# Conditioned block with cached attention and a gated mixer: w4's load keyed apart from w3's, the last tile's norm ahead of the first w2 product's passes, the second pair's attention outputs loaded by halves of heads

## The chip, the cores and the metric

The kernel runs on one core of one Trainium2 chip. The metric is the device time of one launch in microseconds (us); the time of a kernel is the median of its runs. The profile is that of one execution; its span runs from the first to the last instruction.

## What is computed

`x` has 2048 rows of 640. With `D = 640`, 32 heads of 128, 2048 cached keys and values per head and `F = 1728`:

```python
mod = silu(c) @ w_mod                       # six rows: sa, ca, ga, sb, cb, gb
h = layernorm(x) * (1 + ca) + sa
q = (h @ wq) split into 32 heads of 128
o = softmax(q @ k_cache.T * 128**-0.5) @ v_cache
x = x + ga * (o @ wo)                       # wo: 4096 x 640
h = layernorm(x) * (1 + cb) + sb
g = gelu(layernorm(h) @ w1)                 # 640 x 640; then each quarter of the
                                            # columns shifted by 1, -1, 2, -2 rows
x1 = h + shifted(g) @ w2                    # 640 x 640
y = x1 + gelu(layernorm(x1) @ w3) @ w4      # w3: 640 x 1728, w4: 1728 x 640
out = x + gb * y
```

Operands are bf16, sums fp32.

## The kernel before

**Order.** A small planner (`Prog`) takes operations in the order in which the code names them, puts each on its engine's list, and derives the waits from named keys: an operation waits for the last writer of every key it reads or writes, and for the readers of every key it writes. Each engine runs its list in order, and a transfer's wait is taken by the engine that issues it: whatever stands behind it on that engine waits too. There is no other scheduler; the order of the code is the order on every engine.

**Attention.** Most of the time goes into 512 steps (one head, one tile of 128 query rows): scores on PE, minimum and negation on DVE (L584), exponential on ACT (L597), a DMA transpose of the probabilities (L230), and the product with the values on PE (L307). GpSimd normalizes the outputs and writes them to a scratch in DRAM (L462), grouped by pairs of query tiles (tiles 0 and 1 are pair 0, tiles 2 and 3 pair 1, and so on).

**The part behind it.** The 16 tiles of 128 rows pass through these stages. I name them as the code does:

- `load_ot(pr)` (L504): SP issues a DMA transpose that brings a pair's 32 heads (64 blocks of 128 x 128) from the scratch into one of two buffers, `hTx` for even pairs and `negS` for odd ones. Pair 0 comes in three pieces (12, 12 and 8 heads), every other pair in one. The key `("OT", buffer, part)` has three parts, and a whole load writes all three. Pair 1 is issued at L623, behind pair 0's last piece and the first quarter of x (`load_xt(0, 1)`, L622); the rest of x follows at L625, and pair 2 with the loads of w1 and w2 after that (L731 to L734).
- `a_pe(j)` (L523): PE multiplies tile j's 32 heads by `wo`: 32 matmuls of 512 columns and 32 of 128 into one of two PSUM banks (L532). `parts` and `hs` let it do some heads only. A bank comes free when DVE has read it (`a_s1`, L644).
- `a_s1`, `a_s2` (L642, L650): DVE adds the product to x, normalizes, modulates and takes the statistics of the next norm; two small GpSimd operations (`rs_of`, L629) make the reciprocal root.
- `nrm_of(l, j)` (L660): DVE writes the normed tile into one of two buffers (L666), and SP issues a DMA transpose of it into `nT` (L672). l is 1 ahead of w1 and 2 ahead of w3.
- `b_op(cc, n)` (L698): five matmuls of w1 for four tiles (L703) into one of two other PSUM banks, and on ACT the GELU that empties the bank (one to three ACTIVATEs, L711). The first eight of the 20 are placed between parts of the last two tiles' `a_pe` (L742, L745).
- `c_op(j)` (L757): ten matmuls of w2 for a tile (L765), DVE's add (L769), statistics, and `nrm_of(2, j-1)`.
- `d_op` (L774): five matmuls of w3 (L780) and a GELU on ACT; `e_op` (L816): 28 matmuls of w4 (L829), DVE, and the output's store.

**Around the change.** When the last tile's `a_s2` has been listed, GpSimd clears two small pads (L751, L752), and ACT issues the loads of w3 (L753) and of w4's first 13 blocks (L754). Both go into the memory that `wo` held, and both write the key `"wo"`, which every `a_pe` reads. Then come `b_op(1, 3)` and `b_op(1, 4)` (L841), and the loop of L855: `c_op(0)`, `nrm_of(1, 15)` (L858), two `b_op`s, `c_op(1)`, two `b_op`s, `c_op(2)`, the load of w4's last block (L860, on SP, which also writes `"wo"`), one `b_op`, `c_op(3)`, and so on. So on PE the order is b(1,3), b(1,4), c(0), b(2,0), b(2,1), c(1), b(2,2), b(2,3), c(2), b(2,4), c(3), b(3,0), b(3,1), c(4), b(3,2), b(3,3), c(5), b(3,4), c(6), d(0,0). b(3,n) needs `nT` of tiles 12 to 15, d(0,n) needs w3 and `nT` of tiles 0 to 3 in their second form.

Of the kernel before, what the change touches and what calls it, by code (L numbers as in the profile page):

```python
# [123 lines left out]
def bass_adaLN_cond__mha_block_cached__mixer_s_mlp__prompt_kernel(  # L124
# [3 lines left out]
    _, H, SK, DH = A_k_cache.shape  # L128
    FF = B_w3.shape[1]
    assert DH == 128 and D % 128 == 0 and SQ % 512 == 0 and SK == 2048  # L130
    KT = D // 128
    NQT = SQ // 128
    NQC = SQ // 512
    NKT = SK // 128
    NFT = (FF + 127) // 128
    FL = FF - (NFT - 1) * 128
# [9 lines left out]
    with ExitStack() as es:  # L146
# [11 lines left out]
        if True:  # L158
            with ExitStack() as es1:
# [8 lines left out]
                wo = sb1("wo", [128, H, D], BF16)  # L168
# [40 lines left out]
                G = Prog(nc, es1, "a")  # L209

                def load_k(h):
                    hb = h % 2
                    G.dma("sync", lambda e: e.dma_start_transpose(KTs[:, hb], A_k_cache[0, h]), ("k", hb), w=[("KT", hb)])
# [126 lines left out]
                if H > 1:  # L340
                    load_wq(1)
                    load_k(1)
                G.dma("sync", lambda e: e.dma_start(wo[:], A_wo.rearrange("(h p) n -> p h n", p=128)), "wo", w=["wo", "woz"])

                G.op("gpsimd", lambda g: g.memset(ident[:], 0.0), w=["id0"])
                G.op("gpsimd", lambda g: g.memset(ones_f, 1.0), w=["onesf"])
# [2 lines left out]
                     r=["id0"], w=["ident"])  # L349
# [3 lines left out]
                for k in range(KT):  # L353
                    G.op("gpsimd", lambda g, k=k: g.tensor_scalar(out=s_bc[:, k, :], in0=ones_f, scalar1=c_f[:, k:k + 1],
                                                                  scalar2=1.0, op0=ALU.mult, op1=ALU.mult),
                         r=["onesf", "cf"] + WRK, w=[("sbc", k)])
# [129 lines left out]
                w4 = wof[:, KT * NFT * 128:KT * NFT * 128 + NFT * D].rearrange("p (f n) -> p f n", f=NFT)  # L486
# [10 lines left out]
                NEG = [("negS", i) for i in range(3)]  # L497
                KVK = ([("KT", b) for b in range(2)] + [("V", b) for b in range(2)] + [("wq", b) for b in range(2)]
                       + [("QT", b, cc) for b in range(2) for cc in range(NQC)])
                HTK = [("hT", cc, k) for cc in range(NQC) for k in range(KT)]  # L500
# [3 lines left out]
                def load_ot(pr, h0=0, h1=H, part=0):  # L504
                    G.dma("sync", lambda e: e.dma_start_transpose(
                        OTj[pr % 2][:, 2 * h0:2 * h1, :], o_scr[pr, :, h0:h1].rearrange("q h z d -> q (h z d)")),
                          ("ot", pr % 2, part), r=[("osd", pr // 2, hh) for hh in range(h0, h1)],
                          w=[("OT", pr % 2, i) for i in ([part] if h1 - h0 < H else range(3))]
                          + ((HTK if pr == 0 else NEG) if pr < 2 else []))

                def load_xt(c0, c1):
                    G.dma("sync", lambda e: e.dma_start(
                        xt[:, 4 * c0:4 * c1], x2d[c0 * 512:c1 * 512, :].rearrange("(t p) d -> p t d", p=128)),
                        ("xt", c0), w=[("x1", t) for t in range(4 * c0, 4 * c1)] + ringk(XT0 + 4 * c0 * D, XT0 + 4 * c1 * D))
# [4 lines left out]
                def ybank():  # L519
                    yn[0] += 1  # L520
                    return yn[0] % 2

                def a_pe(j, b=None, parts=(0, 1, 2), hs=None):  # L523
                    if b is None:
                        b = ybank()
                    pr, z = divmod(j, 2)
                    h0, h1 = hs or (OTC[parts[0]], OTC[parts[-1] + 1])

                    def f(t):
                        for c0, cw in NC2:  # L530
                            for hh in range(h0, h1):
                                ins = t.matmul(YB[b][:, c0:c0 + cw], OTj[pr % 2][:, 2 * hh + z, :], wo[:, hh, c0:c0 + cw],  # L532
                                               start=(hh == 0), stop=(hh == H - 1))
                        return ins
                    G.op("tensor", f, r=[("OT", pr % 2, i) for i in parts] + ["wo", "woz"], w=[("S", b)])
                    return b

                YB = [Sps[:, 0:1024], Sps[:, 1024:2048]]
                LAG = 4
                for s in range(NG + PVD + LAG):  # L540
                    h, j = divmod(s, NQT)
# [5 lines left out]
                    if s == 3:  # L547
                        G.op("gpsimd", lambda g: g.tensor_scalar(
                            out=mod_bc[:, 2 * D:3 * D], in0=mod_bc[:, 2 * D:3 * D], scalar1=1.0, scalar2=1.0, op0=ALU.add, op1=ALU.mult),
                            r=[("mod", i) for i in range(len(MROW))], w=["mod"])  # L550
                    for half in range(2):
                        if s < NG:
                            qk(s, half)
                        if half == 0 and s in (NG + PVD - 5, NG + PVD - 4):
                            b0 = a_pe(0, None if s == NG + PVD - 5 else b0, (s - NG - PVD + 5,))
                        if half == 0 and s == NG + PVD - 2:
                            b1 = a_pe(1, None, (0,))
# [15 lines left out]
                    if 0 <= g_ < NG and g_ % 2 == 1:  # L573
                        p = g_ // 2
                        G.op("scalar", lambda a, p=p: a.copy(  # L575
                            Of[:, p % 4].rearrange("p z d -> p (z d)")[:, 0:259], PO[:, (p % 2) * 512:(p % 2) * 512 + 259]),
                            r=[("O", p % 2)], w=[("Of", p % 4)])
# [3 lines left out]
                    for half in range(2):  # L581
                        if s < NG:
# [6 lines left out]
                                r=[("S", half)], w=[("negS", s % 3), ("nmh", half, r8)])  # L589
# [3 lines left out]
                    if s < NG:  # L593
                        G.op("gpsimd", lambda g, r8=r8: g.tensor_scalar(  # L594
                            out=nm[:, r8:r8 + 1], in0=nm0[:, r8:r8 + 1], scalar1=nm1[:, r8:r8 + 1], scalar2=None, op0=ALU.min),
                            r=[("nmh", 0, r8), ("nmh", 1, r8)], w=[("nm", r8)])
                        G.op("scalar", lambda a, s=s, r8=r8: a.activation(  # L597
                            Pb[:, s % RP, :], negS[:, s % 3, :], ACT.Exp, bias=nm[:, r8:r8 + 1], scale=-1.0),
                            r=[("negS", s % 3), ("nm", r8)], w=[("Pb", s % RP)])
# [7 lines left out]
                        if h + 1 == H and j in (2, PVD + 1):  # L607
                            i = 0 if j == 2 else 1
# [10 lines left out]
                    if s == NG:  # L619
                        G.op("gpsimd", lambda g: g.memset(mhalf, -0.5), w=["mhalf"] + NEG)  # L620
                        load_ot(0, OTC[2], OTC[3], 2)
                        load_xt(0, 1)  # L622
                        load_ot(1)  # L623
                    if s == NG + 2:
                        load_xt(1, NQC)  # L625
                GELU = ACT.Gelu_apprx_tanh
# [23 lines left out]
                def a_s2(j):  # L650
                    u = j % 2
                    G.op("vector", lambda v: v.scalar_tensor_tensor(out=tmp[:, u], in0=xt[:, j], scalar=mvt[:, 0, j, 0:1],
                                                                    in1=mod_bc[:, 2 * D:3 * D], op0=ALU.subtract, op1=ALU.mult),
                         r=[("x1", j), ("mvt", 0, j), "mod"], w=[("tmp", u)])
                    G.op("vector", lambda v: v.scalar_tensor_tensor(out=xb[:, j], in0=tmp[:, u], scalar=rst[:, 0, j:j + 1],
                                                                    in1=mod_bc[:, D:2 * D], op0=ALU.mult, op1=ALU.add),
                         r=[("tmp", u), ("rst", 0, j), "mod"], w=[("xb", j)] + ringk(XB0 + 2 * j * D, XB0 + 2 * (j + 1) * D))
                    stats_of(1, j, xb[:, j], ("xb", j))

                def nrm_of(l, j):  # L660
                    nrm_v(l, j)
                    n_t(j, l == 1 and j == 0)
# [7 lines left out]
                def n_t(j, first):  # L670
                    b = j % 2
                    G.dma("sync", lambda e: e.dma_start_transpose(nT[:, j], nrm[:, b]), ("nt", b),  # L672
                          r=[("nrm", b)], w=[("nT", j)] + (KVK if first else []))
# [3 lines left out]
                for n in range(KT):  # L677
                    lst = []
                    p = 0
                    while p < 128:  # L680
# [8 lines left out]
                        p = pe_  # L689
# [33 lines left out]

                for i in range(NQT):
                    if i < NQT - 2:
                        b = a_pe(0, b0, (2,)) if i == 0 else a_pe(1, b1, (1, 2)) if i == 1 else a_pe(i)
                    if i == NQT - 3:
                        for z in range(2):
                            G.op("gpsimd", lambda g, z=z: g.memset(us[:, :, z * SQ:z * SQ + 4], 0.0), w=[("usz", z)] + OT0K)  # L729
                    if i % 2 == 1 and (i + 3) // 2 < NQT // 2:  # L730
                        load_ot((i + 3) // 2)  # L731
                    if i == 1:
                        G.dma("sync", lambda e: e.dma_start(w1, B_w1.rearrange("(k p) n -> p k n", p=128)), "w1", w=["w1"] + KVK)
                        G.dma("sync", lambda e: e.dma_start(w2, B_w2.rearrange("(k p) n -> p k n", p=128)), "w2", w=["w2"] + NEG)  # L734
                    if i < NQT - 2:
                        a_s1(i, b)
                    if 1 <= i:
                        a_s2(i - 1)
                    if 2 <= i:
                        nrm_of(1, i - 2)  # L740
                    if i == NQT - 2:
                        b = a_mixed(i, [[(b_op, 0, 0)], [(b_op, 0, 1)], [(b_op, 0, 2)], [(b_op, 0, 3)]])  # L742
                        a_s1(i, b)
                    if i == NQT - 1:
                        b = a_mixed(i, [[(b_op, 0, 4)], [(b_op, 1, 0)], [(b_op, 1, 1)], [(b_op, 1, 2)]])  # L745
                        nrm_of(1, i - 1)
                        a_s1(i, b)
                        a_s2(i)
                w3s = B_w3.rearrange("(k p) n -> p k n", p=128)
                if FL < 128:  # L750
                    G.op("gpsimd", lambda g: g.memset(w3[:, :, FF:NFT * 128], 0.0), w=["w3z", "woz"])  # L751
                    G.op("gpsimd", lambda g: g.memset(w4[:, NFT - 1, :], 0.0), w=["w4z", "woz"])  # L752
                G.dma("scalar", lambda e: e.dma_start(w3[:, :, 0:FF], w3s), "w3", w=["w3", "wo"])  # L753
                G.dma("scalar", lambda e: e.dma_start(w4[:, 0:NFT - 1, :], B_w4[0:(NFT - 1) * 128, :].rearrange("(f p) n -> p f n", p=128)),  # L754
                      "w4", w=["w4", "wo"])

                def c_op(j):  # L757
                    b = ybank()
# [95 lines left out]
                        n -= 1  # L854
                for j in range(NQT):  # L855
                    c_op(j)
                    if j == 0:
                        nrm_of(1, NQT - 1)  # L858
                    if j == 2:
                        G.dma("sync", lambda e: e.dma_start(w4[0:FL, NFT - 1, :], B_w4[(NFT - 1) * 128:FF, :]), "w4b", w=["w4b", "w4z", "wo"])  # L860
                    run_fill(1 if j in (2, 5) else 2)
                nrm_of(2, NQT - 1)
                run_fill(len(fill))
# [30 lines left out]
```

## Time and profile before

| what | value |
|---|---|
| median of 3 runs | 1593.59 us (1592.4 to 1593.86) |
| the profiled execution, its own time | 1592.68 us |
| its span | 1590.9 us |
| granted TensorE clock, mean | 0.994 |
| PE, DVE, ACT, POOL busy | 94%, 88%, 80%, 39% of the span |
| attention steps and what leads to them | 0 to about 1280 us |
| `a_pe` of pairs 1 to 7, with eight `b_op` | 1291.85 to 1422.4 us |
| `c_op`, the other `b_op`, the first `d_op` | 1422.4 to 1486 us |
| the other `d_op` and the `e_op` | 1486 to 1587.7 us |

The time outside the span is 1.78 us. Times in the profile count from the span's start. "SPq" and "ACTq" are the issue of a transfer by SP and ACT, in contrast to the transfer's own time, which ends with its landing. PE is TensorE's matmuls, PEld its weight loads, DVE is VectorE, ACT ScalarE, POOL GpSimd. A bracket behind a line of the timeline tells how long the engine stood idle before it and what ended that.

### The profile page before, as it was taken

How to read it: one execution, taken by the hardware profiler on the slowest of the kernel's cores; microseconds unless marked ns; L12 is line 12 of the kernel's file. 1: busy time of each engine (PE TensorE's matmuls, PEld its weight loads, DVE VectorE, ACT ScalarE, POOL GpSimd, SP SyncE). 2: the span in 40 equal slices, each digit the busy share in tenths (PEclk: the TensorE clock that was granted, in tenths of full speed). 3: DMA queues.
4: the chain of work that ended last, by engine and by line, in shares of the span. 5: the costliest groups of instructions: out<-in, count | busy, mean ns of one | idle time of the engine just before them, and what ended most of it. 6: DMA issues, size and time to landing. Idle time of an engine off the chain costs nothing.

```text
span 1590.9 us, 33555 instructions
## 1 busy us (share of the span) xinstructions
PE 1490.5 (94%) x14071; PEld 910.4 (57%) x13047; DVE 1395.6 (88%) x2463; ACT 1274.5 (80%) x1113; POOL 625.0 (39%) x1396
## 2 busy tenths in 40 slices
PE   5899999999999999999999999999999899989999
PEld 3466556656656556665565565656556555544555
DVE  6999999999999999999999999999999746766535
ACT  4999999999999999999999999999999800024230
POOL 0244444444444444444444444444444423332100
PEclk9999999999999999999999999999999999999999
DMA  9999999999999999999999999999999998723100
GB/s 296 244 235 239 232 230 238 238 238 242 240 238 237 232 242 241 242 238 229 237 249 234 240 240 239 241 242 233 245 234 236 237 261 167 138 79 96 38 26 34
DMA packets 1189403, 338.76 MB, mean 213 GB/s; under 512 B 1169856, under 2 KB 1183232, under 8 KB 1189248
## 3 DMA queue, kind: packets, MB, share of 16 engines
q1 hardware_dynamic: 1180768, 315.49, 100.1%
q0 software_dynamic: 6144, 16.79, 3.5%
q10 hardware_dynamic: 2336, 4.34, 0.8%
q8 instruction: 107, 1.75, 0.4%
q14 instruction: 48, 0.39, 0.1%
HBM read 43.48 MB, written 19.40 MB: 40 GB/s over the span
## 4 chain that ended last, share of the span: by engine, by line
DVE 27%; ACT 26%; PE 21%; DMA 16%; issue 8%; POOL 2%; SPq 0%; ACTq 0%; POOLq 0%; DVEq 0%
DVE negS L584 25%; ACT ring L597 21%; DMA ring<-ring 14%; PE Sps L532 8%; PE Sps L829 4%; ACT ring L270 2%; PE QPp L780 2%; PE Oaug L780 2%; ACT kv L252 1%; ACT Of L575 1%; PE Sps L765 1%; PE PTp L307 1%; POOL small L594 1%; DMA negS<-o_scratch 1%; DVE ring L272 1%
## 5 line engine op out<-in xcount | busy, mean ns | idle before, releaser
L584 DVE TENSOR_SCALAR_CACHE_REDUCE negS<-Sps 128x1024 f32<-128x1024 f32 x1024 | 1179.0, 1220 | 33.5 <-PE Sps L15 32.7
L597 ACT ACTIVATE ring<-negS,small 128x2048 bf16<-128x2048 f32 x512 | 1030.2, 2019 | 23.7 <-POOL small L594 22.1
L307 PEld LDWEIGHTS PTp<-kv,ring 128*128 128x128 bf16 x8192 | 551.8, 98 | 380.9 <-issue 111.8
L307 PE MATMUL PTp<-kv,ring 128*128 128x129 bf16 x8192 | 646.2, 221 | 47.7 <-DMA ring<-ring 47.1
L294 PE MATMUL Sps<-kv 128*128 128x512 bf16 x1024 | 393.7, 384 | 19.6 <-DVE negS L584 15.4
L594 POOL TENSOR_SCALAR small<-small 128x1 f32<-128x1 f32 x512 | 147.1, 287 | 631.4 <-DVE negS L584 631.3
L15 PE MATMUL Sps<-kv 128*128 128x512 bf16 x1024 | 388.4, 379 | 0.0
L455 POOL TENSOR_SCALAR On<-Of,small 128x128 bf16<-128x128 f32 x512 | 191.5, 374 | 13.0
L294 PEld LDWEIGHTS Sps<-kv 128*128 128x128 bf16 x1024 | 98.3, 96 | 112.1 <-DVE negS L584 91.1
L448 POOL TENSOR_TENSOR small<-Of,small 128x4 f32<-128x4 f32 x128 | 133.4, 1042 | 9.0 <-ACT Of L575 9.0
L245 PE MATMUL Oaug<-hTx,kv 128*128 128x512 bf16 x320 | 120.8, 381 | 2.6 <-ACT hTx L399 1.7
L245 PE MATMUL QPp<-hTx,kv 128*128 128x512 bf16 x320 | 120.1, 379 | 1.9 <-ACT hTx L399 1.2
L462 POOL DMA_DIRECT2D o_scratch<-On x128 | 103.1, 806 | 40.8 <-POOL On L455 37.2
L575 ACT COPY Of<-PTp 128x259 f32<-128x259 f32 x256 | 96.4, 376 | 14.3 <-PE PTp L307 14.3
L711 ACT ACT_TABLE_LOAD x1 | 1.3, 1283 | 115.7 <-POOL hTx L729 115.7
L584 DVE DVE_READ_ACCUMULATOR negS<-Sps 128x1 f32 x1024 | 85.6, 84 | 0.0
L630 POOL TENSOR_SCALAR negS<-negS 128x1 f32<-128x1 f32 x48 | 25.0, 520 | 137.8 <-DVE negS L639 137.7
L532 PE MATMUL Sps<-wo,negS 128*128 128x128 bf16 (+1 forms) x512 | 71.4, 299 | 3.7 <-DMA negS<-o_scratch 3.7
L532 PE MATMUL Sps<-wo,hTx 128*128 128x128 bf16 (+1 forms) x512 | 70.7, 299 | 0.0
L270 ACT COPY ring<-Oaug 128x1024 bf16<-128x1024 bf16 x64 | 65.5, 1023 | 0.0
L644 DVE TENSOR_TENSOR ring<-Sps,mod_bc 128x640 f32<-128x640 f32 x16 | 13.2, 825 | 57.5 <-PE Sps L532 36.2
L833 DVE TENSOR_TENSOR ring<-Sps,ring 128x640 f32<-128x640 f32 x15 | 12.4, 824 | 57.4 <-PE Sps L829 57.4
(88 smaller groups left out, 1025.9 us busy)
## 6 DMA issues: line engine op xcount, KB each, us to landing
kv<-in_A_v_cache_dram SPq DMA_DIRECT2D x32, 512.0 KB, 5.1
o_scratch<-On POOLq DMA_DIRECT2D x128, 128.0 KB, 4.0
kv<-in_A_wq_dram SPq DMA_DIRECT2D x32, 160.0 KB, 3.4
wo<-in_A_wo_dram SPq DMA_DIRECT2D x1, 5120.0 KB, 17.0
ring<-ring SPq DMA_TRANSPOSE x256, 7.0
ring<-in_A_x_dram SPq DMA_DIRECT2D x5, 640.0 KB, 7.0
ring<-in_w_mod_dram SPq DMA_DIRECT2D x1, 3200.0 KB, 13.7
out_dram<-wo SPq DMA_DIRECT2D x15, 160.0 KB, 1.8
```

The costliest lines, as they stand in the source:

```text
L15: return t.add_instruction(mybir.InstMatmult(name=t.bass.get_next_instruction_name(), ins=[t.lower_ap(rhs), t.lower_ap(lhsT)], outs=[t.low ...
L245: G.op("tensor", lambda t: t.matmul(JB[jb], wq[:, hb, q, :], hT[:, q, cc * 512:(cc + 1) * 512], start=(q == 0), stop=(q == KT - 1)), r=[(" ...
L294: ins = (t.matmul if c2 == 0 else partial(same_weights, t))(Sps[:, col:col + 512], QT[:, hb, j * 128:(j + 1) * 128], KTs[:, hb, col:col + ...
L307: ins = t.matmul(ob[:, 0:129], PTs[:, b, kt, :], Vaug[:, hb, kt, 0:129], start=(kt == 0), stop=(kt == NKT - 1))
L448: G.op("gpsimd", lambda g: g.tensor_tensor(out=rl[:, 4 * b:4 * b + 4], in0=Of[:].rearrange("p a z d -> p (a z) d")[:, 4 * b:4 * b + 4, 128 ...
L455: G.op("gpsimd", lambda g: g.tensor_scalar(out=On[:, b, z, :], in0=Of[:, 2 * b + z // 2, z % 2, 0:128], scalar1=rl[:, 4 * b + z:4 * b + z ...
L462: G.dma("gpsimd", lambda e: e.dma_start(o_scr[jj // 2:jj // 2 + 2, :, hh].rearrange("a p z d -> p a (z d)"), On[:, b].rearrange("p (a z) d ...
L532: ins = t.matmul(YB[b][:, c0:c0 + cw], OTj[pr % 2][:, 2 * hh + z, :], wo[:, hh, c0:c0 + cw], start=(hh == 0), stop=(hh == H - 1))
L575: G.op("scalar", lambda a, p=p: a.copy(Of[:, p % 4].rearrange("p z d -> p (z d)")[:, 0:259], PO[:, (p % 2) * 512:(p % 2) * 512 + 259]), r= ...
L584: G.op("vector", lambda v, half=half, s=s, r8=r8: v.tensor_scalar(out=negS[:, s % 3, half * 1024:(half + 1) * 1024], in0=Sps[:, half * 102 ...
L594: G.op("gpsimd", lambda g, r8=r8: g.tensor_scalar(out=nm[:, r8:r8 + 1], in0=nm0[:, r8:r8 + 1], scalar1=nm1[:, r8:r8 + 1], scalar2=None, op ...
L597: G.op("scalar", lambda a, s=s, r8=r8: a.activation(Pb[:, s % RP, :], negS[:, s % 3, :], ACT.Exp, bias=nm[:, r8:r8 + 1], scale=-1.0), r=[( ...
```

## The change

Four edits:

1. **Key of w4.** A new key `"wo4"` stands for the part of `wo`'s memory that w4 takes. The first load of `wo` writes it, every `a_pe` reads it, and w4's load writes it in place of `"wo"`. So w4's load waits for the last `a_pe`, as w3's does, and no more for w3's load. The load of w4's last block loses the key `"wo"`.
2. **Norm of tile 15.** `nrm_of(1, 15)` moves from behind `c_op(0)` to right behind `a_s2(15)`. On DVE it then stands ahead of the add and statistics of `c_op(0)`; on SP the order of issues stays as it was.
3. **Pair 1 by halves.** Its load is issued as two DMA transposes of 16 heads (32 blocks) each, the first under part 0 of the key, the second under parts 1 and 2.
4. **Products of tiles 2 and 3.** `a_two` does them as two calls of `a_pe`, heads 0 to 15 behind part 0 and heads 16 to 31 behind parts 1 and 2. The matmuls are the same in number; their order becomes 16 of 512 columns, 16 of 128, 16 of 512, 16 of 128.

```diff
-G.dma("sync", lambda e: e.dma_start(wo[:], ...), "wo", w=["wo", "woz"])
+G.dma("sync", lambda e: e.dma_start(wo[:], ...), "wo", w=["wo", "woz", "wo4"])
...
 def load_ot(pr, h0=0, h1=H, part=0):
...
-          w=[("OT", pr % 2, i) for i in ([part] if h1 - h0 < H else range(3))]
-          + ((HTK if pr == 0 else NEG) if pr < 2 else []))
+          w=[("OT", pr % 2, i) for i in ([part] if pr == 0 else (part, 2)[:part + 1] if h1 - h0 < H else range(3))]
+          + (HTK if pr == 0 else NEG if pr == 1 and part == 0 else []))
...
-        G.op("tensor", f, r=[("OT", pr % 2, i) for i in parts] + ["wo", "woz"], w=[("S", b)])
+        G.op("tensor", f, r=[("OT", pr % 2, i) for i in parts] + ["wo", "woz", "wo4"], w=[("S", b)])
         return b
+
+    def a_two(j):
+        b = a_pe(j, None, (0,), (0, H // 2))
+        return a_pe(j, b, (1, 2), (H // 2, H))
...
         load_xt(0, 1)
-        load_ot(1)
+        load_ot(1, 0, H // 2, 0)
+        load_ot(1, H // 2, H, 1)
...
-        b = a_pe(0, b0, (2,)) if i == 0 else a_pe(1, b1, (1, 2)) if i == 1 else a_pe(i)
+        b = a_pe(0, b0, (2,)) if i == 0 else a_pe(1, b1, (1, 2)) if i == 1 else a_two(i) if i in (2, 3) else a_pe(i)
...
         a_s1(i, b)
         a_s2(i)
+        nrm_of(1, i)
...
 G.dma("scalar", lambda e: e.dma_start(w4[:, 0:NFT - 1, :], ...),
-      "w4", w=["w4", "wo"])
+      "w4", w=["w4", "wo4"])
...
     c_op(j)
-    if j == 0:
-        nrm_of(1, NQT - 1)
     if j == 2:
-        G.dma("sync", lambda e: e.dma_start(w4[0:FL, NFT - 1, :], ...), "w4b", w=["w4b", "w4z", "wo"])
+        G.dma("sync", lambda e: e.dma_start(w4[0:FL, NFT - 1, :], ...), "w4b", w=["w4b", "w4z"])
```

More of the change, by code (lines that the diff above doesn't have):

```diff
@@ L342, in bass_adaLN_cond__mha_block_cached__mixer_s_mlp__prompt_kernel @@
                     load_k(1)
-                G.dma("sync", lambda e: e.dma_start(wo[:], A_wo.rearrange("(h p) n -> p h n", p=128)), "wo", w=["wo", "woz"])
+                G.dma("sync", lambda e: e.dma_start(wo[:], A_wo.rearrange("(h p) n -> p h n", p=128)), "wo", w=["wo", "woz", "wo4"])
                 G.op("gpsimd", lambda g: g.memset(ident[:], 0.0), w=["id0"])
@@ L856, in bass_adaLN_cond__mha_block_cached__mixer_s_mlp__prompt_kernel @@
                     c_op(j)
-                    if j == 0:
-                        nrm_of(1, NQT - 1)
                     if j == 2:
-                        G.dma("sync", lambda e: e.dma_start(w4[0:FL, NFT - 1, :], B_w4[(NFT - 1) * 128:FF, :]), "w4b", w=["w4b", "w4z", "wo"])
+                        G.dma("sync", lambda e: e.dma_start(w4[0:FL, NFT - 1, :], B_w4[(NFT - 1) * 128:FF, :]), "w4b", w=["w4b", "w4z"])
                     run_fill(1 if j in (2, 5) else 2)
```

## The prediction, made before the changed kernel ran

> **What bounds the kernel now.** The clock comes first: 0.994 on average, so it falls somewhere, and the place must be found. Then the chain of work that ended last, in order of time, over the last 320 us:
>
> ```profile
> 1278.22 13.58 DMA negS<-o_scratch
> 1291.80 0.05 issue
> 1291.85 106.67 PE Sps L532 x784
> ...
> 1421.28 1.09 PE Oaug L703 x5
> 1422.37 0.02 issue
> 1422.40 0.01 ACT hTx L711
> 1422.40 9.49 DMA wo<-in_B_w_dram
> 1431.90 0.02 issue
> 1431.92 0.37 ACTq L754
> 1432.29 0.05 issue
> 1432.34 0.59 ACT hTx L711
> ```
>
> Each line has a start, a duration, and what the end of the kernel hung on. From 1291.85 us on that is PE, but for one gap: w3's transfer (1422.40, 9.49 us), behind it ACT's issue of w4 (L754), and behind that a GELU. Before 1291.85 the chain is the load of pair 1. So the change aims at two waits of PE. The list of waits over the rest of the kernel (1437 us to the end) shows none on PE; what is saved at the gaps comes off the end, if nothing else is late. The timeline of PE at the two gaps; the bracket is idle time and what ended it:
>
> ```profile
> 1291.85 17.56 PE L532 MATMUL Sps<-wo,negS 128*128 128x512 bf16 x128 [3.74 <-DMA negS<-o_scratch]
> ...
> 1433.68 2.29 PE L703 MATMUL QPp<-kv 128*128 128x512 bf16 x5 [7.42 <-ACT hTx L711]
> 1435.77 1.65 PE L703 MATMUL Oaug<-kv 128*128 128x512 bf16 x5
> 1437.25 1.52 PE L765 MATMUL Sps<-negS,hTx 128*128 128x512 bf16 x10
> ```
>
> 3.74 us and 7.42 us are lost. And the five matmuls at 1433.68 take until 1435.77, 2.09 us, where five take 1.08 us elsewhere in the chain. The table of stretches explains it (PE clock, then DMA share and GB/s, are the last three columns):
>
> ```profile
> 1426.00:1428.00 2.00, 0.26 (x5) 0.09 (x2) 1.93 (x5) 0.00 (x0) 0.00 (x0) 1.00 1.04 421
> 1430.00:1432.00 2.00, 0.00 (x0) 0.00 (x0) 0.27 (x1) 0.00 (x0) 0.87 (x2) 0.50 0.33 76
> 1434.00:1436.00 2.00, 2.00 (x6) 0.73 (x5) 0.00 (x0) 0.16 (x1) 0.00 (x0) 0.50 0.99 358
> ```
>
> The clock halves while PE stands still and is whole again by about 1437. At the 3.74 us gap it stays at 1.00. Last, the issues on SP around pair 1, with their time on the queue:
>
> ```profile
> 1275.01 2.17 SPq L505 DMA_TRANSPOSE hTx<-o_scratch  x1
> 1277.79 0.38 SPq L512 DMA_DIRECT2D ring<-in_A_x_dram  x1
> 1278.22 11.61 SPq L505 DMA_TRANSPOSE negS<-o_scratch  x1
> 1289.93 0.53 SPq L512 DMA_DIRECT2D ring<-in_A_x_dram  x1
> 1290.55 14.73 SPq L505 DMA_TRANSPOSE hTx<-o_scratch  x1
> ```
>
> The last is pair 2, 64 blocks; the view by line gives it 16.8 us to landing, so 1307.35. The same load alone, at 1326.87, takes 7.81 us to issue. So the stretch from 1278 to 1305 is bound by the transfers, with a DMA share of 1.0 or more.
>
> **Edit 1, the key of w4.** What hangs on ACT's wait: behind L754 stand the GELUs of b(1,3) and b(1,4), which empty the banks that b(2,0) and b(2,1) need. c(0) starts at 1424.74 and takes 1.36 us, b(2,0) and b(2,1) 1.08 each at full clock, so c(1) could start at 1424.74 + 1.36 + 2.16 = 1428.26. It starts at 1437.25. **Lost: 8.99 us**, of which 7.42 is the wait and 1.57 mostly the half clock.
>
> After the edit ACT issues w3 at 1422.40 (0.44 us) and w4 at 1422.84. The GELU of b(1,2) ends at 1423.59, that of b(1,3) (1.20 us) then at 1424.9, that of b(1,4) at 1425.5; PE wants the first bank at 1424.74 + 1.36 = 1426.10. What is late next? All times from here on are without edit 3's shift, which moves them alike.
>
> - *The issue of w4*, right behind w3: 0.37 us behind an idle queue in the trace; the slowest ordinary load on SP, behind others in the first microseconds, takes 3.04. With 3.04 the GELU of b(1,3) ends at 1427.1 and PE loses 1.0. I take 0, by the nearest row: L512 behind a transpose in flight, 0.53 us. Bounds: 0 and -1.0; no gain is possible, since the bank is early.
> - *The PSUM banks of c.* DVE: statistics of tile 15 end at 1427.92; by edit 2 it then waits for GpSimd (1428.84) and norms tile 15 until 1429.5, and c(0)'s add ends at 1430.3. c(2), which needs that bank, starts at 1428.26 + 3.52 = 1431.78. Cover 1.5 us. From then on a tile costs DVE 2.47 us (from the add at 1442.33 to the norm's end at 1444.80) against 2.44 or 3.52 between c's on PE.
> - *Tile 15 in `nT`*, for b(3,0): c(2) at 1431.78, one b and c(3): 1431.78 + 1.36 + 1.08 + 1.36 = 1435.58. The transpose is issued at 1429.5; all others of L672 take 2.6 to 4.1 us to land, the long ones beside the loads of pairs. So 1432.1 to 1433.6: free, with 2 us of cover. If the cover goes, each us costs one.
> - *w3*, for d(0,0): 1454.03 - 8.99 = 1445.04. w3 and w4 one after the other take 9.49 and 7.9 us; together from 1422.40 that is 1439.8 at the latest, unless they slow each other. Free.
> - *`nT` of tile 3 in its second form*, for d(0,0): norm ends at 1450.76 and d(0,0) starts at 1454.03 now, 3.3 us for a landing of 2.6. Both move by 8.99. Free.
> - *w4's last block* (L860, SP): its wait on w4 was over (1431.92 + 7.9 = 1439.8) when SP came to it at 1446.08; nothing gained or lost.
>
> **Edit 2** moves one DVE operation (0.57 us) and one issue that SP makes in the same order. Without it tile 15 would land 0.8 us later, still inside the cover above. I take 0; its ends are the 0.9 us that DVE now waits for GpSimd, as a loss, and nothing as a gain, both inside the covers.
>
> **Edits 3 and 4, pair 1 by halves.** a_pe(1) ends at 1288.10. The first half's issue is half of 11.61, so it ends at 1284.0, and the whole load lands 2.0 us after its issue ends (1291.80 against 1289.83): landing at 1286.0. PE goes on at 1288.10 and has 4.34 us (half of 17.34 / 2) to do; the second half is wanted at 1292.44 and lands at 1291.8. So the 3.74 us go. The matmuls cost no more: the four parts of the mixed tiles take 2.17 us each, 8.68 together, the whole tile 8.67.
>
> But the next load is late then. a_pe(4) would start at 1288.10 + 17.34 = 1305.44, and pair 2 lands at 1307.35, since the transfers, not PE, set its pace. It now starts at 1309.19, so what is left of the gain is 1309.19 - 1307.35 = 1.84. The second transpose also costs an issue of its own: 16 blocks took 2.17 us, 64 took 7.81, so a fixed part of 2.17 - 16 x (7.81 - 2.17) / 48 = 0.29. **Gain: 1.55 us.** Bounds: 3.74 if pair 2 comes early enough, 0 if the second issue costs as much as the whole piece of 16 blocks (2.17). I take 1.55, as both rows are of this very transpose.
>
> The Trainium skill ("DMA: Bandwidth & Descriptors", section "Anatomy of one DMA") gives a DMA about 2 us of fixed cost. If that were paid on the queue, pair 2 would land at 1309.35 and nothing would be gained; the rows above, by which a landing follows its issue while the next one runs, speak for 0.3.
>
> Pair 3 is issued behind the transposed tile 0, which waits for w1 (1310.4): it lands at 1311.72 + 12.0 = 1323.7, wanted at 1307.65 + 17.34 = 1325.0. Free by 1.3 us; a delay of 0.3 fits. Pair 4 is issued when a_pe(5) ends, lands 11.4 us later and is wanted 17.34 us later. Free.
>
> **Sum.** 8.99 + 1.55 = 10.54; 1592.68 - 10.54 = 1582.1 for an execution like the profiled one. The median of the runs shown is 0.91 above it, which gives 1583.0; I say **1582.6**, between the two. A measurement of this kernel tells about 0.2% (3.2 us) from no change.
>
> **The rivals.**
>
> - *The second transpose pays a full piece* (the 2.17 above): edit 3 brings nothing, 1592.68 - 8.99 = 1583.7. For it: the queue is full there. Against: landings trail their issue by 2.0 us only. 15%.
> - *Pair 2 comes in time* and the whole 3.74 are kept: 1592.68 - 8.99 - 3.74 = 1580.0. For it: its issue takes twice the undisturbed time, so some of it is order, not bytes. Against: the bytes ahead of it stay the same. 8%.
> - *The issue of w4 holds ACT* for 3.04 us: 1583.1. 4%.
> - *The transpose of tile 15 waits for both loads.* If the engines took w3's and w4's packets ahead of SP's, it would land at 1439.8 + 2.6 = 1442.4 in place of 1435.58; with another half-clock stretch that is 6.8 + 1.57 lost: 1590.5, within 0.2%. Against: beside w2's load (L734) the transpose of tile 0 took 2.9 us. 4%. The page's section "Queues, rings and completion order" has each DMA engine take turns between the queues by packets, which speaks against it too.
> - *Slower: two loads and the transposes slow each other.* Place: b(3,0). Pair 2 took 16.8 us beside x's load where 11.4 is the undisturbed time, a factor of 1.47. By that w3 and w4 land at 1422.4 + 1.47 x 17.4 = 1448.0, and tile 15, if it comes last, at 1450.6: 15.0 + 1.57 lost, 1592.68 - 10.54 + 16.6 = 1598.7. It decides from a landing at 1435.58 + 10.54 - 1.57 = 1444.6 on. Against: w3's traffic runs at 360 to 420 GB/s and is over by 1430. 2%.
> - *It doesn't do what it says:* w4 keeps a wait that ends as late as w3's landing. Only edit 3 is left: 1591.1. Its readers and writers by the new key are all done when w3 may start, so 1%.
>
> **How the numbers follow.** The forecast has 66%. Faster by over 0.2% are the forecast, the first three rivals: 93%. Within 0.2%: 5%. Slower: 2%. The range goes from the whole 3.74 (1580.0, and a little below) to no gain by edit 3 and 1.0 lost to w4's issue, on the median's level (1584.7 + 0.9): 1579.5 to 1586.0.
>
> **What would show it.** Right: ACT issues w4 within 1 us of w3; no wait of PE on ACT and no clock of 0.50 behind 1420; PE's wait at pair 1 gone, and one of about 1.9 us at a_pe(4), the first products of pair 2. Wrong: a wait of b(3,0) on the transposed tile 15, of d(0,0) on w3, of c(2) on DVE, or of a_pe(6) on pair 3.

## The result and the profile after

| | us |
|---|---|
| before, median of 6 runs | 1593.72 (1590.30 to 1596.19) |
| changed, median of 6 runs | 1584.87 (1580.90 to 1587.65) |
| ratio changed / before | 0.9944, 95% interval 0.9925 to 0.9963 |
| changed, run again beside other kernels | 0.9936, 0.9921 to 0.9951 |
| profiled execution: its own time, its span | 1586.91, 1585.1 |

The changed kernel is 8.9 us faster, with an interval of 6 to 12 us. I begin with the timeline of ACT in the changed kernel (start, duration, operation; the bracket is idle time and what ended it):

```profile
1423.31 0.42 ACTq L759 DMA_DIRECT2D wo<-in_B_w_dram  x1
1423.77 0.54 ACTq L760 DMA_DIRECT2D wo<-in_B_w_dram  x1
1423.91 0.59 ACT L716 ACTIVATE hTx<-Oaug 64x512 bf16<-64x512 f32 x1
1424.53 1.20 ACT L716 ACTIVATE hTx<-QPp 96x512 bf16<-96x512 f32 x2
```

w4 is issued 0.46 us behind w3, in 0.54 us, and the GELU of b(1,3) follows without a wait. The 7.42 us wait of PE on ACT is gone. The timeline of PE at the two places, and at a third:

```profile
1291.44 17.33 PE L532 MATMUL Sps<-wo,negS 128*128 128x512 bf16 x126
1310.37 9.94 PE L532 MATMUL Sps<-wo,hTx 128*128 128x512 bf16 x68 [1.59 <-DMA hTx<-o_scratch]
...
1427.01 1.24 PE L708 MATMUL QPp<-kv 128*128 128x512 bf16 x5
...
1435.34 1.31 PE L771 MATMUL Sps<-negS,hTx 128*128 128x512 bf16 x9
1438.82 1.24 PE L708 MATMUL Oaug<-kv 128*128 128x512 bf16 x5 [2.18 <-issue]
```

Pair 1 (1291.44) is met without a wait, and a_pe(4) waits 1.59 us for pair 2, where about 1.9 was forecast. The wait in the last line was not forecast: at 1438.82 b(3,0) has waited 2.18 us. The view puts that down to "issue", so it does not name a cause; the next two answers do. They are the views by line of the transpose of tile 15 and of w4's load:

```profile
L677 SPq DMA_TRANSPOSE kv<-Of x1: 1201/1201/1201, 1431.0 to 1431.0; - x1
DMA to landing us min/median/max: 7.7/7.7/7.7
```

```profile
L760 ACTq DMA_DIRECT2D wo<-in_B_w_dram x1: 539/539/539, 1423.8 to 1423.8; - x1
DMA to landing us min/median/max: 15.0/15.0/15.0
```

Tile 15 was issued at 1431.0 and landed 7.7 us later, at 1438.7, where before it took 2.6 us. w4 landed at 1423.8 + 15.0 = 1438.8: the same moment. DVE sees it too; it may not write the next norm into that buffer until the transpose has read it:

```profile
1429.78 1.20 DVE L671 TENSOR_SCALAR Of<-ring,negS 128x640 bf16<-128x640 f32 x1 [0.95 <-POOL negS L637]
...
1438.83 0.61 DVE L671 TENSOR_SCALAR Of<-ring,negS 128x640 bf16<-128x640 f32 x1 [1.72 <-DMA kv<-Of]
```

The table of stretches (the PE clock is the third column from the end) shows no half clock behind that wait, nor where the old one stood:

```profile
1430.00:1432.00 2.00, 2.00 (x14) 1.06 (x13) 1.97 (x3) 1.35 (x3) 0.63 (x2) 1.00 1.02 384
1434.00:1436.00 2.00, 1.95 (x13) 0.93 (x12) 1.93 (x6) 0.82 (x2) 1.00 (x2) 1.00 1.09 334
1436.00:1438.00 2.00, 0.64 (x7) 0.35 (x5) 1.07 (x3) 0.00 (x0) 0.72 (x2) 1.00 1.30 245
1438.00:1440.00 2.00, 1.18 (x6) 0.61 (x7) 1.17 (x2) 0.00 (x0) 0.02 (x1) 1.00 0.38 27
```

**Two spans can't simply be subtracted.** The two profiled executions differ by 5.8 us, the medians by 8.9. The last product with the values (L307, 32 matmuls) starts at 1278.46 before and at 1281.15 in the changed kernel, 2.69 us later, though no edit changes what PE does ahead of it. Over all profiled executions of this study that start lies between 1274.07 and 1282.04. So I compare by two stages, each from an event on PE to another:

- *Stage A*, from the start of that last L307 group to that of a_pe(4): 30.78 before, 29.22 in the changed kernel.
- *Stage B*, from the start of b(1,4) to that of d(0,0): 30.38 (1423.65 to 1454.03) and 23.73 (1424.56 to 1448.29).

1.56 and 6.65 us are saved, 8.2 together. They are one execution each; how far stage A varies between executions is told below.

### The profile page after: what moved, and what is told of

The parts are those of the page before. It is cut to its first block, busy times and chain, and to the rows that moved or that the text cites. A ratio compares the mean times of both kernels' runs of the same rounds, so it can differ in the third digit from the quotient of the medians.

```text
span 1585.1 us, 33308 instructions
## 1 busy us (share of the span) xinstructions
PE 1466.2 (92%) x13822; PEld 910.2 (57%) x13047; DVE 1395.5 (88%) x2463; ACT 1275.2 (80%) x1113; POOL 624.6 (39%) x1396
## 4 chain that ended last, share of the span: by engine, by line
DVE 26%; ACT 25%; PE 20%; DMA 17%; issue 9%; POOL 2%; SPq 0%; ACTq 0%; POOLq 0%; DVEq 0%
DVE negS L588 24%; ACT ring L601 20%; DMA ring<-ring 16%; PE Sps L532 7%; PE Sps L835 4%; ACT ring L270 2%; PE Oaug L786 2%; PE QPp L786 2%; PE Sps L771 1%; ACT kv L252 1%; PE PTp L307 1%; ACT Of L579 1%; DMA hTx<-o_scratch 1%; POOL small L598 1%; DVE ring L372 1%
## 5 line engine op out<-in xcount | busy, mean ns | idle before, releaser
L307 PEld LDWEIGHTS PTp<-kv,ring 128*128 128x128 bf16 x8192 | 551.7, 98 | 370.2 <-DMA ring<-ring 95.2
L307 PE MATMUL PTp<-kv,ring 128*128 128x129 bf16 x8192 | 645.5, 220 | 49.5 <-DMA ring<-ring 48.9
L15 PE MATMUL Sps<-kv 128*128 128x512 bf16 x1024 | 387.9, 379 | 14.2 <-DVE negS L588 8.6
L294 PE MATMUL Sps<-kv 128*128 128x512 bf16 x926 | 356.1, 385 | 24.3 <-DVE negS L588 12.8
L245 PE MATMUL Oaug<-hTx,kv 128*128 128x512 bf16 x264 | 100.1, 384 | 4.8 <-DVE hTx L404 4.8
L245 PE MATMUL QPp<-hTx,kv 128*128 128x512 bf16 x259 | 96.7, 378 | 3.2 <-ACT hTx L399 2.5
L532 PE MATMUL Sps<-wo,hTx 128*128 128x512 bf16 (+1 forms) x502 | 69.3, 297 | 2.7 <-DMA hTx<-o_scratch 2.2
```

What stands on the lines that cost most here:

```text
L15: return t.add_instruction(mybir.InstMatmult(name=t.bass.get_next_instruction_name(), ins=[t.lower_ap(rhs), t.lower_ap(lhsT)], outs=[t.low ...
L245: G.op("tensor", lambda t: t.matmul(JB[jb], wq[:, hb, q, :], hT[:, q, cc * 512:(cc + 1) * 512], start=(q == 0), stop=(q == KT - 1)), r=[(" ...
L294: ins = (t.matmul if c2 == 0 else partial(same_weights, t))(Sps[:, col:col + 512], QT[:, hb, j * 128:(j + 1) * 128], KTs[:, hb, col:col + ...
L307: ins = t.matmul(ob[:, 0:129], PTs[:, b, kt, :], Vaug[:, hb, kt, 0:129], start=(kt == 0), stop=(kt == NKT - 1))
```

## The experiments

My theory after the result: the key of w4 brings most of the gain; pair 1's halves bring the rest; and w4's load, now early, delays the transpose of tile 15 until it has landed itself, which costs 2.2 us. The main rival: the transpose is late because of the order on DVE, or because a transpose beside any load takes so long.

**Edit 1 alone**, on the kernel before:

```diff
-      "w4", w=["w4", "wo"])
+      "w4", w=["w4", "wo4"])
```

with the new key at the load of `wo`, at `a_pe` and at w4's last block as in the change.

> Edit 1 alone (w4's key), on the kernel before; the pair loads whole, tile 15's norm behind c(0). My theory: it carries most of the gain. The 7.42 us wait of PE on ACT and the half clock go (8.99), and PE waits about 2.2 us at b(3,0) for tile 15's transpose, as in the changed kernel, because that transpose lands only when w4's load does: about 6.8 us faster, near 1586.9. PE's 3.7 us at pair 1 stay. Rival: the wait at b(3,0) comes from edit 2's new place of the norm (1.20 us long there in place of 0.57); then it is under 1 us here, and the gain 8 to 9 us.

Measured: a ratio to the kernel before of 0.9962 (0.9947 to 0.9978), 6.0 us faster; the medians differ by 6.9. Stage B takes 23.87 us (1428.04 to 1451.91). The wait at b(3,0) is there without edit 2, and with the norm at 0.57 us, so the rival falls:

```profile
1442.44 1.24 PE L703 MATMUL Oaug<-kv 128*128 128x512 bf16 x5 [2.32 <-issue]
```

Tile 15 is issued at 1434.68 and lands at 1442.4; w4 at 1427.26 + 15.1 = 1442.4.

At pair 1, still loaded whole, something else shows, in the stretches of this kernel:

```profile
1292.00:1294.00 2.00, 0.00 (x0) 0.00 (x0) 1.93 (x5) 0.00 (x0) 0.26 (x1) 1.00 1.34 267
1294.00:1296.00 2.00, 1.23 (x4) 0.61 (x6) 0.40 (x1) 0.00 (x0) 1.02 (x2) 0.78 0.85 213
1296.00:1298.00 2.00, 2.00 (x6) 0.76 (x5) 0.00 (x0) 0.00 (x0) 0.00 (x0) 0.50 1.02 360
```

PE waits 4.00 us, and behind that the clock is 0.50: the products of tiles 2 and 3 take 19.02 us in place of 17.3. Stage A takes 32.72 us. In the kernel before, a wait of 3.74 had not moved the clock.

**Edits 3 and 4 alone**: the changed kernel with the first two edits undone.

> Edits 3 and 4 alone (pair 1 by halves), w4's key and the norm's place as before. My theory: 1.0 to 1.8 us faster (about 1592.3): PE's 3.7 us at pair 1 go, and 1.5 to 2.7 us of waiting appear at a_pe(4), since pair 2's landing sets the pace; at w4 the 7.4 us wait and the clock of 0.50 stay. Rival: the halves cost as much on the queue as they save, and the start of a_pe(4) against the last product with the values moves by less than 0.5 us.

Measured: 0.9976 (0.9960 to 0.9991), 3.8 us faster, with an interval of 1.4 to 6.4. With the 6.0 of edit 1 alone that makes 9.8, beside 8.9 and, run again, 10.2 for the changed kernel. The timeline of PE:

```profile
1277.62 2.03 PE L307 MATMUL PTp<-kv,ring 128*128 128x129 bf16 x32
1279.89 7.55 PE L532 MATMUL Sps<-wo,hTx 128*128 128x512 bf16 x55 [0.23 <-DMA hTx<-o_scratch]
1287.50 17.33 PE L532 MATMUL Sps<-wo,negS 128*128 128x512 bf16 x126
1305.69 12.53 PE L532 MATMUL Sps<-wo,hTx 128*128 128x512 bf16 x80 [0.86 <-DMA hTx<-o_scratch]
```

Stage A takes 28.07 us, and a_pe(4) waits only 0.86. Stage B is as before: 30.16 us, with a wait of 6.39 and the half clock. The rival falls; the size was more than I expected. Over the seven profiled executions with pair 1 in halves and x's load whole, stage A takes 27.8 to 29.2 us, 28.4 on average; over the two with a whole pair 1, 30.8 and 32.7. So the halves bring about 2.4 us against the execution without the half clock at pair 1 and 4.4 against the one with it; each of these is a single execution.

**w4's load late**: the changed kernel, with L760 moved behind the first two products of w3:

```diff
     run_fill(1 if j in (2, 5) else 2)
+    if j == 6:
+        G.dma("scalar", lambda e: e.dma_start(w4[:, 0:NFT - 1, :], ...), "w4", w=["w4", "wo4"])
```

> The changed kernel with w4's load issued later, on ACT behind the first two products of w3 (about 1449 us), so that it isn't under way beside the transpose of tile 15. My theory (w4's traffic delays the transpose): it lands within 2.6 to 3 us of its issue, the 2.18 us wait at b(3,0) goes, and the time falls by 2.2 to about 1582.7; w4 still lands before its first use. Rival (w3's own traffic or the late issue is enough): the transpose still takes over 5 us and 1 us or more of the wait stays.

Measured: 0.9922 (0.9906 to 0.9938), median 1579.67. This interval and the changed kernel's (0.9925 to 0.9963) just overlap, so the stages decide. The timeline of PE has no wait at b(3,0):

```profile
1433.49 1.31 PE L769 MATMUL Sps<-negS,hTx 128*128 128x512 bf16 x9
1434.64 1.24 PE L708 MATMUL Oaug<-kv 128*128 128x512 bf16 x5
```

Tile 15 lands 2.6 us after its issue. Stage B takes 21.39 us: 30.38 - 21.39 = 8.99, exactly what the prediction had counted for edit 1. The theory holds, the rival falls.

The delay has not gone, though: it has moved to transposes that no product waits for. The one issued at 1446.81, 0.34 us behind the late load, takes 8.5 us and lands at 1455.3, with w4 at 1455.5; the next takes 5.7. DVE waits 2.0 us for a buffer there, PE not at all.

**Without edit 2**: the changed kernel, with `nrm_of(1, 15)` behind `c_op(0)` again.

> The changed kernel without edit 2 (tile 15's norm behind c(0), as before). My theory: no difference that can be measured (within 0.5 us of the changed kernel): the norm ends about as late as before, since beside GpSimd's clearing of the pads it took 1.20 us in place of 0.57, and the transpose lands with w4's load in either order; the wait at b(3,0) is 2.2 +- 0.4 us. Rival: the transposes follow the issue, and DVE's order decides: the wait at b(3,0) grows by the 0.8 us that the prediction gave edit 2.

Measured: 0.9945 (0.9925 to 0.9965), as the changed kernel. The wait at b(3,0) is shorter than both expected:

```profile
1432.54 1.24 PE L708 MATMUL Oaug<-kv 128*128 128x512 bf16 x5 [1.28 <-issue]
```

Here w4 took only 13.7 us to land (1418.40 to 1432.1), and tile 15, issued at 1425.82, landed 6.6 us later, at 1432.4. So the wait follows w4's landing, not the order on DVE. Edit 2 changes nothing that can be measured.

**w4's load in halves**, blocks 0 to 5 early and 6 to 12 late, in one execution:

> The changed kernel with w4's load cut in two: blocks 0 to 5 where it stood, 6 to 12 behind the first two products of w3. My theory: the transpose of tile 15 lands when the load that is under way ends, so with half the bytes it lands about 3.5 us earlier, some 4 us after its issue in place of 7.7, at the same time as the first half of w4 (within 0.5 us); the wait at b(3,0) is 0. Rival (any weight load beside it costs the transpose a fixed 5 us more): it lands over 6 us after its issue, behind the half's landing.

Measured: the early half, issued at 1416.03, lands 11.2 us later, at 1427.2; tile 15, issued at 1423.26, after 4.6 us, at 1427.9. No wait at b(3,0), stage B 21.39 us. The distance is 0.7 us in place of 0.5, but a fixed cost falls: with half the bytes in its way the transpose is 3.0 us sooner. The execution took 1576.83 us; one time alone does not rank the kernel.

**The pads cleared later**: in the changed kernel GpSimd's two clearings (L757, L758) move behind `c_op(1)`, in one execution (1584.87 us):

> The changed kernel with GpSimd's two clearings of the pads (w3's and w4's) behind c(1) in place of ahead of w3's load, so that they don't run beside the norm of tile 15. My theory: the norm takes 0.57 us in place of 1.20 and the transpose is issued 0.6 us earlier, but still lands with w4's load (within 0.3 us of it): the wait at b(3,0) stays at 1.3 to 2.3 us. Rival (the landing follows the issue): it lands 0.6 us earlier against w4's landing and the wait is 0.6 shorter.

Measured: the norm takes 0.61 us, and the transpose is issued 0.58 us earlier against w4's issue (6.66 us behind it, 7.24 in the changed kernel). It takes 9.0 us to land, at 1435.3; w4 lands at 1419.71 + 15.6 = 1435.3. So an earlier issue brings nothing, and the rival falls. The wait was longer than I expected, and it brought the half clock with it:

```profile
1435.41 2.29 PE L708 MATMUL Oaug<-kv 128*128 128x512 bf16 x5 [2.82 <-issue]
1437.50 1.59 PE L708 MATMUL QPp<-kv 128*128 128x512 bf16 x5
```

Stage B takes 25.73 us: 21.39 + 2.82 + 1.52. Here 2.82 us of waiting were enough, where 3.74 had not been.

**w4 late, and x's later rows in three loads**:

```diff
-    load_xt(1, NQC)
+    load_xt(1, 2)
+    load_xt(3, NQC)
...
     if i % 2 == 1 and (i + 3) // 2 < NQT // 2:
         load_ot((i + 3) // 2)
+        if i == 3:
+            load_xt(2, 3)
```

> The kernel with w4's load late, and x's later rows in three loads in place of one: the second and the last quarter ahead of pair 2, the third quarter behind pair 3, so 0.66 MB less stands ahead of pair 2. My theory (pair 2's landing is set by the bytes ahead of it): it lands 1.5 to 2.5 us earlier, PE's wait at a_pe(4) (0.6 to 1.6 us in the runs so far) goes, and the time falls by about 1 us below that of the kernel with w4 late. Rival (the landing is set by the issue of its 64 blocks, not by the bytes ahead): pair 2 still takes 13 us and more to issue, the wait stays, and the time is the same.

Measured: 0.9910 (0.9890 to 0.9931), median 1578.80. The wait at a_pe(4) is 0.29 us, and stage A takes 27.43 us, against 28.05 with w4 late alone. Pair 2 lands 27.2 us after the last L307 group starts, 27.8 with w4 late alone: 0.6 us earlier, not 1.5 to 2.5. Its issue fell from 13.60 to 12.45 us, so both expectations were half right: the bytes ahead matter, but by less than their share. The times of this kernel and of the one with w4 late are within each other's intervals.

**The changed kernel again**, beside the last three:

> The changed kernel once more, beside the kernel with w4 late and x split: both theories expect 0.9944 of the kernel before, within its interval, and the wait at b(3,0) again 1.3 to 2.3 us, ending with w4's landing.

Measured: 0.9936 (0.9921 to 0.9951); the wait at b(3,0) 2.07 us, the transpose landing at 1430.8 and w4 at 1430.9. As expected.

Of the kernels with six times or more, the one with w4 late and x split has the lowest median. It beats the kernel before clearly; against the changed kernel, run beside it, it stands at 0.9910 (0.9890 to 0.9931) to 0.9936 (0.9921 to 0.9951), and these intervals just overlap. What the profiles show plainly is stage B: 21.39 us in place of 23.62 and 23.73.

## Why the prediction was right, and its step that failed

- **Edit 1, the key of w4: mechanism right, 8.99 right for what it frees.** Every kernel with w4's load late or cut has a stage B of 21.39. But the changed kernel keeps 23.73: 2.2 of the 2.3 us between them go into a new wait.
- **The step that failed: the landing of tile 15 in `nT`, "1432.1 to 1433.6: free, with 2 us of cover".** I bounded it by the transposes of L672 in the trace of before, 2.6 to 4.1 us. The 4.1 belongs to transposes issued towards the end of a pair's load; none had been issued with 7 us of a load still ahead of it. Those rows already showed what was to come: pair 4 lands at 1326.87 + 11.4 = 1338.3, and the transpose issued at 1334.72 lands at 1338.7, behind it. And the row that I held against a delay, tile 0's 2.9 us beside w2's load, had only 2.2 us of that load left: w2 lands at 1305.97 + 6.7 = 1312.7, the transpose at 1313.4. The runs showed that the transpose lands when the load lands, so the right bound was the load's end: 15.0 us after w4's issue. PE paid 2.18 us for it. I had this as a rival ("the transpose of tile 15 waits for both loads"), at 4%, with the loads one after the other (9.49 + 7.9 = 17.4 us from 1422.40). What it says came true, and its price was too high: issued together, both loads are down 15.5 us after w3's issue, the transpose lands with them and not 2.6 us behind, and no half clock followed in the changed kernel.
- **The issue of w4:** 0.54 us, by the nearest row, as forecast. It cost nothing.
- **Edit 2:** no effect, as forecast, but not for the reason given. I had the norm end at 1429.5; beside GpSimd's clearing of the pads it took 1.20 us in place of 0.57, so the issue came hardly earlier.
- **Edits 3 and 4: mechanism right, the term too small.** PE's wait of 3.74 goes and one at a_pe(4) comes, as said. I put 1.55 for the rest; stage A gives 1.56 between the two profiled executions, which is luck: on average it is 2.4, and more where the wait at pair 1 had brought the half clock with it. Pair 2's landing was not as fixed as I had it; a_pe(4) waits 0.3 to 1.6 us. Nor does the first half come when I had it: I put its landing 7.8 us behind its issue, by half of the whole load's time; it takes 9.6 to 11.2 us, and in three of the seven executions PE waits 0.3 to 0.8 us for it.
- **The second transpose's cost:** the two halves are issued in 11.28 us together with edits 3 and 4 alone and in 13.18 in the changed kernel, the whole load in 11.61 and 12.33. My 0.29 can't be told from nothing. The Trainium skill ("DMA: Bandwidth & Descriptors", "Anatomy of one DMA") gives its 2 us for the path of GpSimd's DMAs, and says that completion, not setup, makes up most of them; so it is no reason to charge them to SP's queue, as the prediction's other sum had it. They are not paid there: pair 2 lands 28.9 us after the start of the last L307 group in both executions with a whole pair 1, and 27.6 to 29.0 us after it in the seven with halves.
- **The sum:** 10.54 forecast; 8.9 measured between the medians. The two misses, -2.2 and about +0.9, explain 1.3 of the 1.7 us between them; the rest is inside the interval of 6 to 12. The median of 1584.87 lies in the range, 2.3 us above the forecast; that it lies no farther off is in part luck, since the two misses have opposite signs.
- **Covers that held:** the banks of c, w3 for d(0,0) (landed 9.4 us after its issue), pair 3, and the second form of `nT`: no PE wait at any of them.

## What to carry to other kernels

When a load is freed to start earlier, ask what else will be under way on the DMA engines in its new place; a small transfer that somebody waits for soon can be held until the large one has landed, so the large one belongs where nothing small is urgent, if its own user is far away. Look at what it then holds up in its new place. Bound such a landing by the end of the load beside it, not by the longest landing that the old trace happens to hold. And where executions of one kernel differ by several us, compare two profiles stage by stage, between two events on the engine that sets the end.

## What the runs showed of the hardware that I had not expected

- **A small DMA transpose issued behind a large load lands with it.** Tile 15's transpose (128 x 640, bf16, on SP's queue) was issued 6.7 to 7.4 us behind w4's load (2.1 MB, on ACT's queue). Landings of the two: 1438.7 and 1438.8, 1442.4 and 1442.4, 1432.4 and 1432.1, 1435.3 and 1435.3, 1430.8 and 1430.9, and with half of w4 1427.9 and 1427.2. The next transpose in the changed kernel, run again, issued 4.2 us later, landed 4.0 us after its issue, 0.5 us behind w4. A load issued behind the transpose does less: with edits 3 and 4 alone w4 is issued 0.57 us behind it, and the transpose lands after 5.2 us, 4.6 us ahead of w4; in the kernel before w4 is issued 1.6 us behind it, and it takes 2.6. With w4 late, and only the last 1.5 to 1.9 us of w3's load beside it, it takes 2.5 to 2.6 us. The packet counts by queue show where the time goes: in the changed kernel ACT's queue moves 1174 packets between 1431.0 and 1434.9, and SP's none; in all five executions with the whole of w4 ahead, SP's first packet comes 3.9 to 4.1 us after the issue. The Trainium skill ("DMA: Bandwidth & Descriptors", "Queues, rings and completion order") says that each engine takes turns between the queues that it has work for, packet by packet; for these 3.9 us no turn of SP's queue is seen, so that rule alone does not bound the landing. What holds the packets back was not tried and stays open.
- **The half clock does not follow from the length of a wait.** Behind the attention, PE waits of 2.82, 4.00, 6.39 and 7.42 us brought it, one of 3.74 did not. It cost 1.5 to 2.4 us on top of the wait. In the attention, near 224 us, waits of 1.90 us (kernel before), 2.08 (without edit 2) and 2.33 (x split) are followed by a clock of 0.50 too, others of 1.6 to 2.1 there are not, nor is one of 3.12 at 457 us (edit 1 alone). The Trainium skill ("TensorE: Matmul & The Clock Gate", Part 1) has activity judged in windows of about 3.4 us that run on by themselves, so that the phase matters, and puts the half clock behind an idle window. Waits of 2.82 us and less hold no such window, so here one that was busy in part was enough; how busy it may be, no run shows.
- **DVE's norm beside a GpSimd memset took 1.20 us in place of 0.57** (1.19 to 1.20 in five executions, 0.61 when the memsets were moved), while the batch-norm statistics (0.89 us for a pair) took no longer beside the same memsets in the kernel before. Why the one is slowed and the other not was not tried.
